# A four-layer attention stack on one core: more exponentials on VectorE in the last layer, and transposes and row sums in column strips

## The chip, the cores and the metric

The kernel runs on one core of a Trainium2 chip. TensorE (PE) multiplies matrices into PSUM, ScalarE (ACT) computes the exponentials, VectorE (DVE) copies, masks and scales, GpSimd (POOL) prepares weights and some masks, and DMA queues move data. The metric is the time of one execution on the device in microseconds. Before the change it is 2272.32 us, the median of three runs (2268.7 to 2274.12).

## The reference

Four layers, A, B, A, B, each with a residual. 2048 tokens, 640 features, 32 heads of 20. A looks at the last 256 keys, B at all keys.

```python
def layer(x, wqkv, wo, window):        # A: window = 256, B: none; S = 2048, D = 640, H = 32, Dh = 20
    h = (x - mean(x)) / sqrt(var(x) + 1e-5)
    q, k, v = split(h @ wqkv)           # each H x S x Dh
    scores = einsum("hqd,hkd->hqk", q, k) * Dh ** -0.5
    scores = where(allowed, scores, -1e9)   # A only
    p = softmax(scores)
    o = einsum("hqk,hkd->hqd", p, v)
    return x + o.reshape(S, D) @ wo
# x -> A -> B -> A -> B
```

The bulk of the work is the exponential of B's scores: 32 x 2048 x 2048 of them in each of two layers.

## The kernel before

**Tiling.** Queries go in four chunks of 512 (c = 0 to 3), heads in eight groups of four (g = 0 to 7). A *unit* is one layer, chunk and group, in the code (l, c, g) with l = 0 to 3. A *bank* is one PSUM bank of 128 x 512: the scores of one head j of the group for one block kc of 128 keys against the 512 queries. A B unit has 16 key blocks x 4 heads = 64 banks. Three banks (sometimes four) make a *tile*. For a tile t, TensorE writes the scores (L1305), ScalarE takes the exponential of the whole tile in one instruction (L1336), and two ticks later TensorE multiplies the result with the values (L1369) into the accumulator bank `op`. Score tiles alternate between PSUM banks 0 to 2 and 3 to 6, so TensorE can be one tile ahead of ScalarE and no more.

**The order is written out by hand.** A loop over t, one *tick* each, emits the scores, the exponential, then as much other work as a budget of credits allows (`pump`: layer norms, projections, value blocks, outputs, the tails of finished units), then the value matmuls. Each engine executes its own instructions in that order. Before a bank is reused, TensorE waits for its reader. Where TensorE would be too quiet, `keep_clock` adds filler matmuls of the identity with a mask (`unread`, L297), to keep its clock up.

**Column strips.** Most full-height matmuls are split by `by_columns` (L292 to L297) into four, each with 32 of the 128 stationary columns, so that they write four strips of 32 partitions. The profile shows their shape as 128\*32. Score matmuls use 32 rows (32\*128), value matmuls 21 columns (128\*21). Some steps use the whole width (128\*128): the transposes of the normed rows (L432, five for each 128 tokens, 300 in all), the row sums of finished units (L1042, eight for a pair of units), and a small transpose of their reciprocals (L1059, 128\*64).

**Exponentials on VectorE.** A unit can set a few banks *aside* (L678): VectorE computes them with bit operations and a polynomial (`t_side`, from L886), two banks (a *pair*) at a time: twice L909 (reads a score bank), L914, L919, L924, L928, L932, L940. In layer 1, from chunk 1 on, two banks of a unit are set aside; in layer 3, from (1, 1) on, four, which are the last key block of the four heads. In layer 3 their scores go to PSUM bank 6 by a matmul of their own (L902), on odd ticks when the side program asks for it. A tile of four banks uses bank 6 too, so it is only made when the side program does not. `SIDE_RATE` is the credit that the side program gets for each tile in the final stretch, 0.85; its steps cost 0.7 or 1.2 credits. Results go to buffers in `ka_all` that the last layer does not need otherwise (`side["out"]`), and their value matmuls (L1378) are the last of the unit. `side_need` (L972) and `side_done` (L990) make sure that the scores and the results are there in the program before they are used.

**Tail of a unit.** `finish_unit` copies `op` out (L856). For each pair of units `t_tail` sums the rows (L1042), takes reciprocals (L1047), splits them in two bf16 parts (L1051, L1052), transposes them (L1059, L1063), spreads them (L1080) and scales the outputs (L1084).

Of the kernel before, what the change touches and what calls it, by code (L numbers as in the profile page):

```python
# [9 lines left out]
BF16 = mybir.dt.bfloat16  # L10
# [5 lines left out]
P = 128  # L16
# [4 lines left out]
NT = S // P  # L21
KD = D // P
G = 8
C = 512
# [4 lines left out]
VW = DH + 1  # L29
# [4 lines left out]
LOG2E = 1.4426950408889634  # L34
EA, EB, EC, ED = -0.10468731, 1.17604568, 0.83196789, 0.24582313
KA = 18
SIDE_RATE = 0.85
QA = 4

PARTS = {  # L40
# [6 lines left out]
def kernel(  # L47
# [10 lines left out]
    nc = tc.nc  # L58
# [7 lines left out]
    big = pool("big", 1)  # L66
# [25 lines left out]
    ident = big.tile([P, P], BF16, name="ident", tag="ident")  # L92
# [6 lines left out]
    qts = [big.tile([P, C], BF16, name=f"qt{n}", tag=f"qt{n}") for n in range(4)]  # L99
    ka_all = big.tile([P, KA, C], BF16, name="ka", tag="ka")  # L100
    kas = [ka_all[:, n, :] for n in range(KA)]
    qas = [big.tile([P, C], BF16, name=f"qa{n}", tag=f"qa{n}") for n in range(QA)]

    ps = psp.tile([P, 8, C], F32, name="ps", tag="ps")
    op = ps[:, 7, :]
# [284 lines left out]
    def t_ln(l, c):  # L390
        while ("x", l, c) not in ready:
            yield ("wait", 1)
        yield from room("xnT", "ln")
        for n in (1, 0):
            order = worder[l, n]
            if order and not any(e in wtiles for e in order):
                wtiles[order[0]] = get_w(*order[0])
        users[l, c] = 9 if (l, c) == (0, 0) else (11, 12, 11, 11)[l]
        mv = mvs.pop((l, c))
        rstd = lnp.tile([P, 4], F32, name="rstd", tag="rstd")  # L400
        nc.gpsimd.tensor_scalar(  # L401
            out=rstd[:], in0=mv[:, :, 1], scalar1=EPS, scalar2=1.0, op0=ALU.add, op1=ALU.mult
        )
        nc.gpsimd.tensor_tensor(out=rstd[:], in0=rstd[:], in1=nhalf[:], op=ALU.pow)
        yield ("wait", 2)
        nmr = lnp.tile([P, 4], F32, name="nmr", tag="nmr")
        nc.vector.scalar_tensor_tensor(
            out=nmr[:], in0=mv[:, :, 0], scalar=-1.0, in1=rstd[:], op0=ALU.mult, op1=ALU.mult
        )
        xt = xtp.tile([P, KD, C], BF16, name="xnT", tag="xnT")  # L410

        def normed(i):
            xn = xnp.tile([P, D], BF16, name="xn", tag="xn")
            nc.vector.tensor_scalar(
                out=xn[:], in0=x_sb[:, 4 * c + i, :],
                scalar1=rstd[:, i : i + 1], scalar2=nmr[:, i : i + 1],
                op0=ALU.mult, op1=ALU.add,
            )
            return xn

        rows = deque([normed(0)])
        yield ("wait", 1)
        for i in range(4):
            if i < 3:
                rows.append(normed(i + 1))
            xn = rows.popleft()
            mb = yield from take_m()
            for _ in range(1+(l<2)):
                unread(mb)
            trp = ps[:, mb, :].bitcast(BF16)[:, 0 : KD * P].rearrange("p (c m) -> p c m", c=KD)  # L430
            for dc in range(KD):
                nc.tensor.transpose(  # L432
                    out=trp[:, dc, :], in_=xn[:, dc * P : (dc + 1) * P], identity=ident[:]
                )
            evac(xt[:, :, i * P : (i + 1) * P], trp)
            drop_m(mb)
            yield ("pe", 0.4)
        xnT[l, c] = xt
        live["ln"] -= 1
        ready.add(("xnT", l, c))  # L440
# [227 lines left out]
    class Unit:  # L668
        def __init__(self, l, c, g, part=None):
            self.l, self.c, self.g, self.part = l, c, g, part  # L670
            self.windowed = l % 2 == 0
            self.aside = ()
            if self.windowed:
                sets = [(m, b0, subs, j) for m, b0, subs in window_banks(c) for j in range(4)]
            else:

                if c > 0 and (l, c, g) != (3, 1, 0):
                    self.aside = (2, 3) if l == 1 else (0, 1, 2, 3)  # L678
                k0, k1 = key_blocks(l, part)
                sets = [  # L680
                    (None, 0, [(kc, 0, 4, 0)], j) for kc in range(k0, k1) for j in range(4)
                    if kc < NT - 1 or j not in self.aside
                ]
            n = len(sets)
            self.banks = [
                (self, j, m, b0, subs, i < 4, i >= n - 4 + len(self.aside), i == n - 1)
                for i, (m, b0, subs, j) in enumerate(sets)
            ]
# [179 lines left out]
    def side_start():  # L868

        assert live["xnT"] == 0  # L870
        tl = [xtp.tile([P, KD, C], BF16, name="xnT", tag="xnT") for _ in range(3)]
        live["xnT"] += 3
        f = [v[:, 0:4, :].rearrange("p a b -> p (a b)") for v in tl[0:3]]
        side["tiles"] = [v.bitcast(F32) for v in f]
        side["out"] = deque(ka_all[:, KA - 6 + 2 * n : KA - 4 + 2 * n, :] for n in range(3))
        side["late"] = True

    def side_early():
# [9 lines left out]
    def t_side():  # L888

        V = nc.vector  # L890
        while aside:
            u = aside[0]
            for pair in range(len(u.aside) // 2):
                while id(u) not in loaded or (u.l == 3 and not side["late"]):
                    yield None
                for i in range(2):
                    yield "bank"
                    xi, xm, xw = side["tiles"]
                    if u.l == 3:
                        mseq[0] += 1  # L900
                        mfree[6] = (state["tick"] + 2, mseq[0])
                        nc.tensor.matmul(  # L902
                            ps[:, 6, :], lhsT=u.k(NT - 1, u.aside[2 * pair + i]),
                            rhs=u.q(u.aside[2 * pair + i], 0, 4), start=True, stop=True,
                        )
                        side["psum"] = ps[:, 6, :]
                    scored = side.setdefault("scored", {})
                    scored[id(u)] = scored.get(id(u), 0) + 1
                    V.tensor_scalar(  # L909
                        out=xi.bitcast(I32)[:, i * C : (i + 1) * C], in0=side["psum"],  # L910
                        scalar1=SCALE * LOG2E * E23, scalar2=-128.0 * E23, op0=ALU.mult, op1=ALU.max,
                    )
                    yield 0.7
# [59 lines left out]
    def side_need(u):  # L973

        if u.l == 3:
            n = 0
            while u in aside and side.get("scored", {}).get(id(u), 0) < 4:
                n += 1
                assert n < 10000
                side["credit"] = max(side["credit"], 0.1)  # L980
                if side_step(mfree[6][0] <= state["tick"]):
                    continue
                t = choose(False)
                if t is None:
                    state["tick"] += 1
                else:
                    advance(t)
# [35 lines left out]
    def t_tail(us):  # L1023
# [15 lines left out]
        for i, (l, c, g, oT) in enumerate(us):  # L1039
            for qb in range(4):  # L1040
                a = 16 * i + 4 * qb
                nc.tensor.matmul(  # L1042
                    zp[:, a : a + 4], lhsT=oT[:, qb * P : (qb + 1) * P],
                    rhs=sel4[:], start=True, stop=True,
                )
        rz = rzp.tile([P, 2, 16], F32, name="rz", tag="rz")[:, 0:n, :]
        nc.vector.reciprocal(out=rz.rearrange("p u r -> p (u r)"), in_=zp)  # L1047
        drop_m(mb)
# [7 lines left out]
        mb = yield from take_m()  # L1056
        warm_bank(mb)
        rp = ps[0 : 32 * n, mb, :].bitcast(BF16)[:, 0:P]
        nc.tensor.transpose(  # L1059
            out=rp, in_=hl.rearrange("p u n r -> p (u n r)"), identity=ident[:]  # L1060
        )
        rT = rzp.tile([64, P], BF16, name="rT", tag="rT")
        nc.vector.tensor_copy(out=rT[0 : 32 * n], in_=rp)  # L1063
        drop_m(mb)
# [130 lines left out]
    with tc.manual_schedule():  # L1195
# [17 lines left out]
        while n < last_layer:  # L1213
            size = 2 if len(tiles) % 2 and narrow(banks[n][0]) else 3
            u = banks[n][0]
            at = placed.setdefault(id(u), [])
            extra = []
            if u.aside and len(at) < 2 and banks[n + 1][0] is u and len(tiles) >= 3 * len(at) + (at or [0])[0]:

                extra = [(u, u.aside[len(at)], "side", 0, [(NT - 1, 0, 4, 0)], False, False, False)]  # L1220
                at.append(len(tiles))
                size = 2
            for b in banks[n : n + size]:
                starts.setdefault(id(b[0]), len(tiles))
            tiles.append(banks[n : n + size] + extra)
            n += size
# [41 lines left out]
        while ended is None or t < ended + 8:  # L1268
# [84 lines left out]
            for n in range(2 if n_b == 0 or t > closed + 1 else 0):  # L1353
                u = pts[0][3][0] if pts else None
                size = 4
                if u is not None and u.aside and pts[0][3][4][0][0] == NT - 1:
                    size -= len(u.aside)
                if len(pts) < size or pts[size - 1][0] > t - n - (3 if u.windowed else 2):
                    break
                group = [pts.popleft() for _ in range(size)]  # L1360
# [13 lines left out]
                        )  # L1374
                if end and u.aside:
                    pair = side_done(u)
                    for n, j in enumerate(u.aside):
                        nc.tensor.matmul(  # L1378
                            op[32 * j : 32 * j + VW, :], lhsT=u.v(NT - 1, j),
                            rhs=pair[n // 2][:, n % 2, :], start=False, stop=True,  # L1380
                        )
                    side["out"].extend(pair)
                if end:
# [72 lines left out]
```

The softmax here doesn't subtract the row's maximum and nothing guards it: scores larger than these inputs give would overflow.

## Time and profile before

| | |
|---|---|
| time | 2272.32 us (2268.7 to 2274.12, three runs) |
| profiled run | 2268.72 us, span 2267.0 us |
| granted TensorE clock | 0.993 of full |
| exponentials on ScalarE (L1336) | 1636 instructions, 2089.3 us busy |
| VectorE's exponentials in layer 3 (L909 to L940) | 92 bank reads, 46 pairs |
| transposes of normed rows (L432) | 300, 28.4 us busy |
| row sums (L1042) | 512, 22.7 us busy |
| small transposes (L1059) | 64, 15.5 us busy |
| filler matmuls (L297, masks and ident) | 6452, 553.2 us busy |

A busy time of an engine counts each moment once, so matmuls that run side by side in four strips have a busy time well under their count times their mean. The page's slices divide the span in 40 equal parts of 56.7 us; layer 3 fills about the last thirteen.

### The profile page before, as it was taken

How to read it: one execution, taken by the hardware profiler on the slowest of the kernel's cores; microseconds unless marked ns; L12 is line 12 of the kernel's file. 1: busy time of each engine (PE TensorE's matmuls, PEld its weight loads, DVE VectorE, ACT ScalarE, POOL GpSimd, SP SyncE). 2: the span in 40 equal slices, each digit the busy share in tenths (PEclk: the TensorE clock that was granted, in tenths of full speed). 3: DMA queues.
4: the chain of work that ended last, by engine and by line, in shares of the span. 5: the costliest groups of instructions: out<-in, count | busy, mean ns of one | idle time of the engine just before them, and what ended most of it. 6: DMA issues, size and time to landing. Idle time of an engine off the chain costs nothing.

```text
span 2267.0 us, 65801 instructions
## 1 busy us (share of the span) xinstructions
PE 1973.3 (87%) x28523; PEld 776.0 (34%) x28524; DVE 1269.8 (56%) x2158; ACT 2166.5 (96%) x1740; POOL 326.2 (14%) x571
## 2 busy tenths in 40 slices
PE   8999998988888888888888988898888888888887
PEld 3444343334333333333333443342322222222222
DVE  6766575435554565555564644442566666656665
ACT  7789899999999989999899999999999999999998
POOL 4454334201100122001210022002000000000000
PEclk9999999999999999999999999999999999999999
DMA  6233223422210233002330033103211111111100
GB/s 195 72 91 94 74 87 93 100 76 50 78 34 15 60 88 104 17 28 58 93 90 15 16 106 105 31 17 91 65 51 31 31 40 34 31 31 43 42 21 16
DMA packets 88384, 136.80 MB, mean 60 GB/s; under 512 B 20766, under 2 KB 63486, under 8 KB 88094
## 3 DMA queue, kind: packets, MB, share of 16 engines
q1 hardware_dynamic: 68878, 79.43, 12.6%
q0 software_dynamic: 19216, 53.17, 8.0%
q8 instruction: 223, 3.65, 0.7%
q14 instruction: 67, 0.55, 0.1%
HBM read 99.52 MB, written 27.79 MB: 56 GB/s over the span
## 4 chain that ended last, share of the span: by engine, by line
ACT 49%; PE 23%; issue 17%; DVE 9%; POOL 1%; DMA 1%; SPq 0%; ACTq 0%; DVEq 0%; POOLq 0%
ACT pt L1336 47%; PE ps L297 14%; PE ps L1305 5%; PE ps L1369 2%; DVE pt L1416 1%; ACT ka L1336 1%; DVE x_sb L562 1%; DVE st L320 1%; DVE on L1084 1%; PE ps L432 1%; PE ps L1080 0%; DVE vs L320 0%; DVE va L320 0%; PE ps L1042 0%; DVE raw_o L909 0%
## 5 line engine op out<-in xcount | busy, mean ns | idle before, releaser
L1336 ACT ACTIVATE pt<-ps 128x1536 bf16<-128x1536 f32 (+2 forms) x1636 | 2089.3, 1462 | 64.8 <-PE ps L1305 56.2
L297 PE MATMUL ps<-masks,ident 128*32 128x512 bf16 x6452 | 553.2, 388 | 113.2 <-ACT pt L1336 59.1
L1305 PE MATMUL ps<-qt,kt 32*128 32x512 bf16 x4004 | 545.7, 384 | 85.5 <-ACT pt L1336 77.6
L1369 PE MATMUL ps<-pt,vt 128*21 128x512 bf16 x3844 | 392.2, 382 | 0.1
L1305 PEld LDWEIGHTS <-kt 32*128 32x128 bf16 x4004 | 163.4, 91 | 544.1 <-issue 526.8
L297 PEld LDWEIGHTS <-ident 128*32 128x32 bf16 x6452 | 162.0, 94 | 361.6 <-issue 350.4
L1416 DVE TENSOR_TENSOR pt<-pt,masks 128x1024 bf16<-128x1024 bf16 (+6 forms) x331 | 191.0, 604 | 154.9 <-ACT pt L1336 154.1
L297 PE MATMUL ps<-xnT,wqk 128*32 128x512 bf16 x3320 | 221.7, 385 | 17.1 <-DVE st L320 7.9
L320 DVE CAST st<-ps 128x512 bf16<-128x512 f32 x134 | 92.6, 691 | 188.1 <-PE ps L297 187.7
L909 DVE TENSOR_SCALAR xnT<-ps 128x512 int32<-128x512 f32 x92 | 63.6, 691 | 191.4 <-PE ps L902 191.3
L297 PE MATMUL ps<-wop,on 128*32 128x320 bf16 x3712 | 156.9, 301 | 13.3 <-DVE x_sb L562 8.4
L1305 PE MATMUL ps<-qa,ka 32*128 32x384 bf16 (+2 forms) x1408 | 117.9, 276 | 32.0 <-ACT pt L1336 29.4
L1369 PEld LDWEIGHTS <-vt 128*21 128x21 bf16 x3956 | 102.5, 91 | 110.4 <-issue 64.8
L1084 DVE TENSOR_TENSOR on<-on,ps 128x512 bf16<-128x512 bf16 x128 | 86.3, 683 | 67.0 <-PE ps L1080 65.3
L297 PE MATMUL ps<-wv,xnT 128*32 128x320 bf16 x2560 | 112.4, 301 | 10.8 <-DVE on L1084 3.3
L297 PEld LDWEIGHTS <-wqk 128*32 128x32 bf16 x3320 | 79.1, 96 | 112.8 <-issue 59.4
L562 DVE TENSOR_TENSOR x_sb<-x_sb,ps 128x320 bf16<-128x320 bf16 x120 | 58.0, 483 | 104.9 <-PE ps L297 104.7
L297 PEld LDWEIGHTS <-on 128*32 128x32 bf16 x3712 | 92.8, 96 | 65.9 <-issue 49.2
L856 DVE CAST on<-ps 128x512 bf16<-128x512 f32 x112 | 77.0, 687 | 59.9 <-PE ps L1378 32.9
L401 POOL TENSOR_SCALAR rstd<-mv 128x4 f32<-128x4 f32 x15 | 3.8, 253 | 712.4 <-DVE mv L388 702.8
L1305 PEld LDWEIGHTS <-ka 32*128 32x128 bf16 x1408 | 43.2, 92 | 117.0 <-issue 110.9
L1369 PE MATMUL ps<-pt,va 128*21 128x384 bf16 (+2 forms) x1408 | 76.9, 281 | 4.6 <-POOL pt L1406 3.5
(100 smaller groups left out, 1589.8 us busy)
## 6 DMA issues: line engine op xcount, KB each, us to landing
vt<-v_d SPq DMA_DIRECT2D x48, 336.0 KB
kt<-k_d SPq DMA_DIRECT2D x192, 80.0 KB
wqk<-in_B_wqkv_dram POOLq DMA_DIRECT2D x80, 160.0 KB, 3.6
wqk<-in_A_wqkv_dram POOLq DMA_DIRECT2D x70, 160.0 KB, 3.3
k_d<-st POOLq DMA_DIRECT2D x75, 128.0 KB, 2.2
q_d<-st POOLq DMA_DIRECT2D x75, 128.0 KB, 2.2
qt<-q_d SPq DMA_DIRECT2D x384, 20.0 KB
v_d<-vs POOLq DMA_DIRECT2D x16, 336.0 KB, 3.4
```

Of the source, the lines that this page charges most:

```text
L297: nc.tensor.matmul(out_[r], lhsT=lhsT[:, r], rhs=rhs, start=start, stop=stop)
L320: nc.vector.tensor_copy(out=out_, in_=in_)
L401: nc.gpsimd.tensor_scalar(out=rstd[:], in0=mv[:, :, 1], scalar1=EPS, scalar2=1.0, op0=ALU.add, op1=ALU.mult)
L432: nc.tensor.transpose(out=trp[:, dc, :], in_=xn[:, dc * P : (dc + 1) * P], identity=ident[:])
L562: nc.vector.tensor_tensor(out=xv, in0=had, in1=yp, op=ALU.add)
L856: nc.vector.tensor_copy(out=oT, in_=op)
L909: V.tensor_scalar(out=xi.bitcast(I32)[:, i * C : (i + 1) * C], in0=side["psum"], scalar1=SCALE * LOG2E * E23, scalar2=-128.0 * E23, op0=AL ...
L1084: nc.vector.tensor_tensor(out=oT, in0=oT, in1=zb, op=ALU.mult)
L1305: nc.tensor.matmul(sp[:, i, col * P : (col + qn) * P], lhsT=u.k(kc, j), rhs=u.q(j, q0, qn), start=True, stop=True,)
L1336: nc.scalar.activation(out=pt[:, i:k, b0 * P :], in_=sp[:, i:k, b0 * P :], func=ACT.Exp, scale=SCALE,)
L1369: nc.tensor.matmul(op[32 * j : 32 * j + VW, q0 * P : (q0 + qn) * P], lhsT=u.v(kc, j), rhs=pg[:, i, col * P : (col + qn) * P], start=(first ...
L1416: nc.vector.tensor_tensor(out=pt_[:, i:k, cols], in0=pt_[:, i:k, cols], in1=mv_, op=ALU.mult)
```

## The change

It has three parts. First, in layer 3, chunks 1 and 2, units with odd g set six banks aside in place of four: the two more are heads 0 and 1 of key block 14. Each of these eight units so has three pairs on VectorE. To make room in the order, the side program's credit for a tile goes from 0.85 to 1.1, and the four tiles `qa`, which become one tile `qa_all`, serve as two more result buffers. Second, the transposes of the normed rows are issued as four strips of 32 columns each, 20 for 128 tokens in place of five, and the small transpose as one strip for each unit. Third, the row sums go through `by_columns`, 32 narrow matmuls for a pair of units in place of eight.

```diff
-SIDE_RATE = 0.85
+SIDE_RATE = 1.1
...
-    qas = [big.tile([P, C], BF16, name=f"qa{n}", tag=f"qa{n}") for n in range(QA)]
+    qa_all = big.tile([P, QA, C], BF16, name="qa", tag="qa")
+    qas = [qa_all[:, n, :] for n in range(QA)]
...
             for dc in range(KD):
-                nc.tensor.transpose(
-                    out=trp[:, dc, :], in_=xn[:, dc * P : (dc + 1) * P], identity=ident[:]
-                )
+                for j in range(4):
+                    a = dc * P + 32 * j
+                    nc.tensor.transpose(
+                        out=trp[32 * j : 32 * j + 32, dc, :], in_=xn[:, a : a + 32],
+                        identity=ident[:],
+                    )
...
-                    self.aside = (2, 3) if l == 1 else (0, 1, 2, 3)
+                    self.aside = tuple((NT - 1, j) for j in ((2, 3) if l == 1 else range(4)))
+                    if l == 3 and (c < 3 and g % 2):
+                        self.aside += ((NT - 2, 0), (NT - 2, 1))
...
         side["out"] = deque(ka_all[:, KA - 6 + 2 * n : KA - 4 + 2 * n, :] for n in range(3))
+        side["out"].extend(qa_all[:, 2 * n : 2 * n + 2, :] for n in range(2))
...
-                nc.tensor.matmul(
-                    zp[:, a : a + 4], lhsT=oT[:, qb * P : (qb + 1) * P],
-                    rhs=sel4[:], start=True, stop=True,
-                )
+                by_columns(zp[:, a : a + 4], oT[:, qb * P : (qb + 1) * P], sel4[:], True, True)
...
-        nc.tensor.transpose(
-            out=rp, in_=hl.rearrange("p u n r -> p (u n r)"), identity=ident[:]
-        )
+        for i in range(n):
+            nc.tensor.transpose(
+                out=rp[32 * i : 32 * i + 32], in_=hl[:, i].rearrange("p n r -> p (n r)"),
+                identity=ident[:],
+            )
```

The rest of the diff carries the key block along with the head of a bank set aside, in the scores, in the count that `side_need` asks for and in the value matmuls.

More of the change, by code (lines that the diff above doesn't have):

```diff
@@ L677, in __init__ @@
                 if c > 0 and (l, c, g) != (3, 1, 0):
-                    self.aside = (2, 3) if l == 1 else (0, 1, 2, 3)
+                    self.aside = tuple((NT - 1, j) for j in ((2, 3) if l == 1 else range(4)))
+                    if l == 3 and (c < 3 and g % 2):
+                        self.aside += ((NT - 2, 0), (NT - 2, 1))
+                    if l == 1 and 0:
+                        self.aside += ((NT - 1, 0), (NT - 1, 1))
                 k0, k1 = key_blocks(l, part)
@@ L681, in __init__ @@
                     (None, 0, [(kc, 0, 4, 0)], j) for kc in range(k0, k1) for j in range(4)
-                    if kc < NT - 1 or j not in self.aside
+                    if (kc, j) not in self.aside
                 ]
@@ L901, in t_side @@
                         mfree[6] = (state["tick"] + 2, mseq[0])
+                        kc, j = u.aside[2 * pair + i]
                         nc.tensor.matmul(
-                            ps[:, 6, :], lhsT=u.k(NT - 1, u.aside[2 * pair + i]),
-                            rhs=u.q(u.aside[2 * pair + i], 0, 4), start=True, stop=True,
+                            ps[:, 6, :], lhsT=u.k(kc, j), rhs=u.q(j, 0, 4), start=True, stop=True
                         )
@@ L976, in side_need @@
             n = 0
-            while u in aside and side.get("scored", {}).get(id(u), 0) < 4:
+            while u in aside and side.get("scored", {}).get(id(u), 0) < len(u.aside):
                 n += 1
@@ L1217 @@
             extra = []
-            if u.aside and len(at) < 2 and banks[n + 1][0] is u and len(tiles) >= 3 * len(at) + (at or [0])[0]:
-                extra = [(u, u.aside[len(at)], "side", 0, [(NT - 1, 0, 4, 0)], False, False, False)]
+            if (
+                len(at) < len(u.aside) and banks[n + 1][0] is u
+                and len(tiles) >= 3 * len(at) + (at or [0])[0]
+            ):
+                kc, j = u.aside[len(at)]
+                extra = [(u, j, "side", 0, [(kc, 0, 4, 0)], False, False, False)]
                 at.append(len(tiles))
@@ L1355 @@
                 size = 4
-                if u is not None and u.aside and pts[0][3][4][0][0] == NT - 1:
-                    size -= len(u.aside)
+                if u is not None:
+                    size -= sum(kc == pts[0][3][4][0][0] for kc, _ in u.aside)
                 if len(pts) < size or pts[size - 1][0] > t - n - (3 if u.windowed else 2):
@@ L1376 @@
                     pair = side_done(u)
-                    for n, j in enumerate(u.aside):
+                    for n, (kc, j) in enumerate(u.aside):
                         nc.tensor.matmul(
-                            op[32 * j : 32 * j + VW, :], lhsT=u.v(NT - 1, j),
-                            rhs=pair[n // 2][:, n % 2, :], start=False, stop=True,
+                            op[32 * j : 32 * j + VW, :], lhsT=u.v(kc, j),
+                            rhs=pair[n // 2][:, n % 2, :], start=False,
+                            stop=all(jj != j for _, jj in u.aside[n + 1 :]),
                         )
```

## The prediction

> **What bounds the kernel now.** First the summary by engine and the slices of the span, to find the engine that is nowhere short of work.
>
> ```profile
> PE 1973.3 (87%) x28523; PEld 776.0 (34%) x28524; DVE 1269.8 (56%) x2158; ACT 2166.5 (96%) x1740; POOL 326.2 (14%) x571
> ...
> DVE  6766575435554565555564644442566666656665
> ACT  7789899999999989999899999999999999999998
> ```
>
> ScalarE (ACT) is full except in the first tenth of the span and in a few later slices. In the last third VectorE (DVE) is at six tenths: this is where it takes over exponentials. Next the stages (us, then busy time of PE, weight loads, DVE, ACT, POOL):
>
> ```profile
> 100.00:300.00 200.00, 184.42 (x3276) 85.46 (x3279) 129.58 (x259) 171.81 (x161) 85.47 (x157) 0.97 0.30 86
> ...
> 1530.00:1775.00 245.00, 207.86 (x2657) 69.84 (x2648) 123.23 (x167) 243.40 (x179) 14.02 (x20) 0.99 0.20 57
> 1775.00:2015.00 240.00, 204.21 (x2554) 64.08 (x2546) 148.45 (x185) 239.97 (x176) 0.00 (x0) 1.00 0.12 34
> 2015.00:2258.00 243.00, 206.88 (x2495) 65.51 (x2493) 149.27 (x190) 239.69 (x176) 0.00 (x0) 0.99 0.10 29
> ```
>
> The last three stretches are roughly chunks 1, 2 and 3 of the final layer. ScalarE is idle for 0.03 us of the 240 of chunk 2: there a microsecond less of exponentials is a microsecond less of time, if nothing else becomes late. From 100 to 300 us ScalarE is idle for 28 us and TensorE is busy for 184 of 200: there TensorE sets the pace. The list of waits names it: ScalarE's longest wait, over the whole span and then from 1600 to 2250 us, is for the score matmuls.
>
> ```profile
> ACT pt L1336 <- PE ps L1305: 56.2, 114, 2.2
> ...
> DVE xnT L909 <- PE ps L902: 191.3, 89, 5.2
> ...
> ACT pt L1336 <- PE ps L1305: 2.0, 5, 0.9
> ```
>
> The first line is the whole span, the other two the final layer. There ScalarE waits for only 2.0 us, and VectorE stands idle for 191 us before reading a score bank (L909), because the planner releases that step late and not because VectorE is short of time.
>
> **What the Trainium skill says.** "TensorEngine Tiling (Array Packing)", Key Properties: going from one tiling mode to another drains TensorE, going between tiles of one mode does not. The trace agrees:
>
> ```profile
> 758.91 0.40 PE L297 MATMUL ps<-masks,ident 128*32 128x512 bf16 x4
> 759.24 0.45 PE L432 MATMUL ps<-ident,xn 128*128 128x128 bf16 x5
> 759.63 0.40 PE L1369 MATMUL ps<-pt,vt 128*21 128x512 bf16 x4
> ...
> 1699.94 0.40 PE L297 MATMUL ps<-masks,ident 128*32 128x512 bf16 x4
> ...
> 1700.17 0.39 PE L1369 MATMUL ps<-pt,vt 128*21 128x512 bf16 x4
> ```
>
> Four column strips (128*32) are followed by other strips (128*21) after 0.23 us, but by a full-width transpose (128*128) after 0.33: a drain of 0.10 us. The five transposes hold TensorE for 0.39 us; at the 56 ns between their starts in the records they need 5 x 0.056 = 0.28, so the way back costs about 0.1 as well. "TensorE: Matmul & The Clock Gate", Part 3, says that matmuls on different strips run side by side, about 4 ns apart; Part 1 of that page ("Wait — 56ns, not 53.3ns?") says that starts never come closer than about 25 ns however narrow the matmul. For strips these two disagree. The trace speaks for the first at 128 columns:
>
> ```profile
> 703.18 0.39 PE L1369 MATMUL ps<-pt,va 128*21 128x384 bf16 x8
> 703.50 0.39 PE L1305 MATMUL ps<-qa,ka 32*128 32x384 bf16 x6
> ```
>
> Eight strips (four of 128 columns, four of 384, as window groups are built) took 0.32 us with the drain behind them, which is what one strip of 128 and one of 384 need. Nothing in the trace shows 32 strips of four columns in a row.
>
> **The change part by part.**
>
> *Fewer exponentials on ScalarE.* Units of chunks 1 and 2 with odd g, eight units, hand VectorE two more banks each, 16 banks. By the instruction order of both programs this removes two activations of 2048 columns, three of 1536 and one of 512, and adds one of 1024:
>
> ```profile
> L1336 ACT ACTIVATE pt<-ps 128x1536 bf16<-128x1536 f32 x1361 | 1875.1, 1560 | 56.5 <-PE ps L1305 49.7 <-issue 2.9 <-DVE on L1084 0.5
> ...
> L1336 ACT ACTIVATE ka<-ps 128x2048 bf16<-128x2048 f32 x28 | 56.0, 1998 | 0.0
> ```
>
> 2 x 1.998 + 3 x 1.560 + 0.680 - 1.068 = **8.3 us** (0.680 and 1.068 are the means of 512 and 1024 columns). All of it lies where ScalarE is never idle, so all of it counts. Four-bank tiles cost less per bank and become two fewer through the denser side work; that is in the sum.
>
> *More work on VectorE.* Eight more pairs. A pair is two bank reads (0.691), two bit operations (0.694) and four polynomial steps (1.22): 1.38 + 1.39 + 4.88 = 7.65 us, 61 us in all, over some 485 us of chunks 1 and 2. VectorE's 272 busy us there become 333, 69%. It has the time. The rate of 1.1 credits a tile (a credit is about a microsecond by these rows) against 1.56 us a tile leaves 0.46 us a tile for the 2 to 3 us of other work per unit of 20 tiles.
>
> *Lateness of the side results.* TensorE takes the pairs in the last matmuls of a unit (L1378), and behind that matmul stand the next score matmuls, for which ScalarE waits. In the program order the last step of a unit's last pair stands, before, 22 tiles ahead of that use in chunk 1 and 8 at the end of chunk 3. After, the reserve shrinks at odd units of chunk 2 to 4, 2, 1 and 0 tiles, then recovers in chunk 3. Only unit (2,7) is short: its last score is issued in tile 1470, its use ends tile 1473, some 3.6 tiles or 5.6 us later, while bank read, bit operations and polynomial need 0.69 + 1.39 + 4.88 = 7.0 us. TensorE stands about 1.4 us, of which the score tile in reserve (one activation, 1.56, less the tile's own TensorE work of about 0.9) hides half: **+0.8 us**, between 0 and 2.5.
>
> *Transposes in strips (L432, 60 groups of five become 20).* At 56 ns for four strips the groups keep their 0.28 us and lose the drains: all 60 follow strips, 45 precede strips, so 105 drains of 0.1, 10.5 us of TensorE. If starts were bound at 25 ns, 20 x 0.025 = 0.5 us would eat the gain. *The small transposes (L1059, 65)* lose a drain ahead 45 times and behind 51 times, 10 us. *Row sums (L1042, 65 groups)*: eight matmuls 25 ns apart become 32. Lower bound eight times 25 ns, a gain of up to two drains, 0.17 us a group; upper bound 32 x 0.025 = 0.8 us, a loss of 0.43. I take 0.3 to 0.4 us, no gain. What counts is only where ScalarE waits. Of the 60 transpose groups, 33 have a ScalarE gap within 4 us behind them; taking at most 0.2 us of it each, 6.3 us. The same count gives 16 and 2.5 us for the small transposes, 14 and 2.2 us for the row sums. Of the 8.8 us without row sums I take half, because a gap is often set by a chain of filler and projection matmuls that the next wait stretches again: **-4 us**.
>
> *At no cost:* one tile qa in place of four (the waits of its loads are the same in both programs), and 32 filler matmuls fewer among 6452.
>
> Sum: 2272.3 - 8.3 + 0.8 - 4 = 2260.8.
>
> **The rivals.**
> - *Only ScalarE's relief counts*: the TensorE time freed from drains turns into waits elsewhere (VectorE's evacuations, L320). For it: 27 of 60 transposes and 49 of 65 tails have no ScalarE gap behind them. 2272.3 - 7.5 = 2264.8.
> - *Everything counts*, as the time freed before 400 us adds up from group to group: 2272.3 - 8.3 - 9 = 2255.
> - *Strips are bound by issue*, 25 ns each: transposes gain nothing, row sums lose 0.43 us at the 15 places with a gap, 6.5 us. 2272.3 - 7.5 + 6.5 = 2271. Against it the eight strips above; for it, that the densest microsecond of the trace holds 68 TensorE instructions, and the new row sums would pass 64 in a third of that.
> - *VectorE becomes late*: L909 must free bank 6 before TensorE's next side score (L902), and TensorE is in order. If each of the 2 x 54 side scores of the final layer held the scores behind it by 0.12 us, 13 us: 2272.3 - 8.3 - 1 + 13 = 2276, and slower still, 2280, if the odd units' last pairs come late too. Against it: 31% of VectorE free.
>
> **How the numbers follow.** Forecast 0.54, only ScalarE 0.14, everything 0.13, issue-bound 0.11, VectorE late 0.08. The predicted time is 2261. The lower end, 2253, takes in the full gain; the upper, 2271, takes in the issue-bound case and leaves out late VectorE. Faster by over 0.2% means under 2267.8: the first three cases, 0.81, less 0.02 for the spread of 5 us between runs of before. Slower (over 2276.9): half of the last case and a little of the fourth, 0.06.
>
> **What would show it.** Right: in chunks 1 and 2 ScalarE stays over 99% busy and ends some 8 us sooner; VectorE near 69% there; next to no wait of L1378 for VectorE except near the end of chunk 2; the transposes follow fillers after 0.23 us. Wrong: row sums that hold TensorE for over 0.5 us; ScalarE waiting for scores in the final layer for more than 4 us; no fewer ScalarE gaps before 400 us.

## The result and the profile after

The changed kernel takes 2261.48 us (median of four runs, 2259.42 to 2264.71), before 2273.11 beside it: a ratio of 0.9954, with an interval of 0.9935 to 0.9973. In a second measurement on another chip (e11_after below) the ratio was 0.9977, 0.9967 to 0.9988. So the change is worth 5 to 10 us. The forecast was 2261. As the experiments show, this hit is luck: it is the sum of two large terms that were both wrong, in opposite directions.

The page's summary and slices of the changed kernel, in the order of those of before:

```profile
PE 1947.9 (86%) x30990; PEld 775.5 (34%) x30991; DVE 1328.4 (59%) x2222; ACT 2158.6 (96%) x1735; POOL 325.7 (14%) x571
...
DVE  6766675436464556455563644442577777776774
ACT  7789899999999999999899999999999999999998
```

VectorE gained 58.6 us of work, about what was worked out (61), and is now at seven tenths in the final layer. ScalarE lost 7.9 us. TensorE is busy for 25 us less with 2467 matmuls more: those are strips that run side by side and drains that are gone. The stages, with two stretches that hold about the same work as before (us, then PE, weight loads, DVE, ACT, POOL):

```profile
100.00:300.00 200.00, 183.47 (x3790) 88.25 (x3785) 133.09 (x267) 176.36 (x165) 87.39 (x160) 0.98 0.32 89
...
1765.00:2005.00 240.00, 204.40 (x2674) 63.32 (x2671) 178.65 (x218) 238.72 (x175) 0.00 (x0) 1.00 0.13 36
```

From 100 to 300 us ScalarE works 176.4 us, not 171.8: it is better fed. In chunk 2, where it lost 0.03 us of 240 before, it now loses 1.3 with less to do. The waits say the same. The first line is the whole span, the others are from 1600 to 2250 us:

```profile
ACT pt L1347 <- PE ps L1316: 58.0, 117, 2.5
...
DVE xnT L918 <- PE ps L912: 138.6, 95, 3.2
...
ACT pt L1347 <- PE ps L1316: 8.0, 13, 2.5
...
PE ps L1389 <- DVE ka L949: 2.6, 1, 2.6
```

In the final layer ScalarE waits 8.0 us for scores in place of 2.0, ahead of it 50.0 in place of 54.2 (58.0 - 8.0 against 56.2 - 2.0). A new line has come in: TensorE waits 2.6 us for the last polynomial step of one pair. To compare kernels I use one mark, the start of ScalarE's 1250th instruction (counted from zero, the load of its function table left out), just before the final stage; ScalarE's instructions up to it are the same in all kernels here. In the profiles of before and after it lies at 1583.8 and 1573.2 us, and from there to ScalarE's end it takes 672.1 and 674.0 us. In these two profiles all that was gained came ahead of the mark, and the stage for which the exponentials were taken away became 1.9 us longer.

### The profile page after: what moved, and what is told of

Same layout as the page of the kernel before. It is cut to its first block, busy times and chain, and to the rows that moved or that the text cites. A ratio compares the mean times of both kernels' runs of the same rounds, so it can differ in the third digit from the quotient of the medians.

```text
span 2258.4 us, 70795 instructions
## 1 busy us (share of the span) xinstructions
PE 1947.9 (86%) x30990; PEld 775.5 (34%) x30991; DVE 1328.4 (59%) x2222; ACT 2158.6 (96%) x1735; POOL 325.7 (14%) x571
## 4 chain that ended last, share of the span: by engine, by line
ACT 47%; PE 22%; issue 16%; DVE 13%; POOL 1%; DMA 1%; ACTq 0%; SPq 0%; DVEq 0%; POOLq 0%
ACT pt L1347 45%; PE ps L298 14%; PE ps L1316 5%; PE ps L1380 2%; DVE pt L1428 1%; ACT ka L1347 1%; DVE st L321 1%; DVE on L1092 1%; DVE x_sb L566 1%; DVE va L321 1%; PE ps L1088 1%; DVE xnT L937 1%; DVE xnT L933 1%; DVE xnT L941 0%; PE ps L435 0%
## 5 line engine op out<-in xcount | busy, mean ns | idle before, releaser
L298 PEld LDWEIGHTS <-ident 128*32 128x32 bf16 x6420 | 166.7, 94 | 363.1 <-issue 349.7
L298 PE MATMUL ps<-wop,on 128*32 128x320 bf16 x3712 | 156.9, 301 | 14.4 <-DVE x_sb L566 8.7
L918 DVE TENSOR_SCALAR xnT<-ps 128x512 int32<-128x512 f32 x108 | 74.7, 692 | 141.6 <-PE ps L912 138.6
L298 PEld LDWEIGHTS <-on 128*32 128x32 bf16 x5760 | 116.7, 95 | 76.9 <-issue 54.8
L298 PEld LDWEIGHTS <-xnT 128*32 128x32 bf16 x2560 | 63.7, 96 | 49.1 <-issue 38.0
```

What stands on the lines that cost most here:

```text
L298: nc.tensor.matmul(out_[r], lhsT=lhsT[:, r], rhs=rhs, start=start, stop=stop)
L918: V.tensor_scalar(out=xi.bitcast(I32)[:, i * C : (i + 1) * C], in0=side["psum"], scalar1=SCALE * LOG2E * E23, scalar2=-128.0 * E23, op0=AL ...
```

## The experiments

Percentages are against the kernel before on the same chip; us are the percentage of 2271. "Final" is the stretch from the mark to ScalarE's end in the profiled run, "idle" ScalarE's gaps in it, "waits" what TensorE waited for VectorE from 1585 to 2250 us, "half clock" how long the trace shows a granted TensorE clock of 0.5 in the final stretch.

| kernel | time against before, interval | us | final | idle | waits | half clock |
|---|---|---|---|---|---|---|
| before | | | 672.1 | 2.3 | 6.8 | 6.8 |
| after, first | -0.46% (-0.65, -0.27) | -10.4 | 674.0 | 9.4 | 19.5 | 13.6 |
| e11_after | -0.23% (-0.33, -0.12) | -5.2 | 675.5 | 10.3 | 19.3 | 20.4 |
| e1_strips | -0.37% (-0.55, -0.19) | -8.4 | 672.8 | 2.9 | 7.2 | 10.2 |
| e2_side | +0.02% (-0.09, +0.13) | +0.5 | 673.5 | 8.6 | 18.3 | 13.6 |
| e3_no_late | -0.38% (-0.51, -0.25) | -8.6 | 671.6 | 6.6 | 14.3 | 10.2 |
| e4_rate | +0.05% (-0.06, +0.17) | +1.1 | 681.5 | 9.8 | 14.4 | 25.7 |
| e5_trans | -0.30% (-0.40, -0.20) | -6.8 | 670.5 | 1.1 | 7.1 | 3.4 |
| e6_tails | -0.17% (-0.30, -0.05) | -3.9 | 671.6 | 2.0 | 7.4 | 7.1 |
| e7_hold | -0.35% (-0.50, -0.20) | -7.9 | 670.1 | 1.5 | 5.7 | 3.4 |
| e8_fill | -0.18% (-0.28, -0.08) | -4.1 | 675.8 | 4.6 | 11.1 | 3.4 |
| e9_c1_hold | -0.41% (-0.57, -0.26) | -9.3 | 672.2 | 5.1 | 10.2 | 13.6 |
| e10_gap | -0.77% (-0.99, -0.54) | -17.5 | 665.5 | 1.2 | 0 | 3.4 |
| e12_gap_only | -0.47% (-0.63, -0.30) | -10.7 | 671.5 | 1.9 | 0.2 | 6.8 |

Ahead of the mark the ten kernels with all the strips issue the same instructions in the same order on TensorE, VectorE and ScalarE, and yet their profiles reach it between 1571.0 and 1583.7 us. The granted clock goes with this spread: e1_strips, the earliest, has 10 us at half clock ahead of the mark, e9_c1_hold, the latest, 41. So one profile alone can't size the strips; for them the timed runs count. These spread in the same way: of the 34 runs of before beside e10_gap, the fastest (2263.5 us) has a mean granted clock of 0.996, the slowest (2279.4 us) 0.988. The final stage of four-bank kernels whose waits for VectorE are short (7.4 us or less) repeats within 3 us (670.1 to 672.8).

**Which part brought the gain: e1_strips, e2_side.** e1 is the kernel before with the diff's strips alone, e2 is the changed kernel with the strips undone:

```diff
# e1_strips, on before                      # e2_side, on after
+ four strips in t_ln (L432)                - four strips in t_ln
+ by_columns(zp...) in t_tail (L1042)       - by_columns(zp...)
+ one strip for each unit (L1059)           - one strip for each unit
```

> The kernel before with the strips alone (transposes, row sums and small transposes); the last layer's sharing of exponentials as before. Theory A (the strips brought nearly all of the gain: at one point of ScalarE's work, its 1250th instruction, the changed kernel is 10.6 us ahead, and after that it only loses): 2262 to 2263, 10 to 11 us under before, and the final layer from that point lasts 672 us as before. Theory B (the strips are worth the 4 us of the prediction, and the rest of the difference between the two profiles is the spread of runs): 2269.

> The kernel before with the sharing alone (six banks at odd units of chunks 1 and 2, rate 1.1, one qa tile), transposes and row sums full-width. Theory A (the ScalarE time saved is spent on stalls behind the late pair of unit (2,7) and its neighbours): 0 to 2 us over before, 2273 to 2275, with a ScalarE gap of about 2.5 us near the end of chunk 2 and TensorE's value matmuls of that unit waiting for VectorE. Theory B (the relief is worth its 7.5 us): 2265.5.

The strips give 8.4 us, the sharing nothing that can be measured (+0.5, between -2.0 and +3.0). Theory A holds in direction; it put the strips at 10 to 11 by one pair of profiles, two over the measured size but inside its interval (4.3 to 12.5). Two pairs of profiles with equal time at half clock ahead of the mark agree: e7_hold reaches it 7.6 us sooner than before (23.9 us at half clock in both), the changed kernel 7.4 us sooner than e2_side (17.1 in both). The sum of e1 and e2, -7.9, lies between the two measurements of the whole change. The strips do what the drains promised. In the changed kernel:

```profile
752.54 0.40 PE L298 MATMUL ps<-masks,ident 128*32 128x512 bf16 x4
752.76 0.45 PE L435 MATMUL ps<-ident,xn 128*32 128x128 bf16 x20
753.04 0.39 PE L1380 MATMUL ps<-pt,vt 128*21 128x512 bf16 x4
...
2038.25 0.40 PE L298 MATMUL ps<-masks,ident 128*32 128x512 bf16 x4
2038.47 0.39 PE L298 MATMUL ps<-sel,on 128*32 128x4 bf16 x32
2038.70 0.41 PE L1380 MATMUL ps<-pt,vt 128*21 128x512 bf16 x4
```

The start column is what to read. Fillers to transposes: 0.22 us, not 0.33. Twenty strips of a transpose group: 0.28, where the five full-width ones with their drain held 0.39. The 32 row sums with four columns each take 0.23 us, with no drain ahead of them (fillers to row sums 0.22). In the kernel before, the eight full-width ones took 0.28, and a drain of 0.1 ahead of them:

```profile
1046.43 0.40 PE L297 MATMUL ps<-masks,ident 128*32 128x512 bf16 x4
1046.76 0.35 PE L1042 MATMUL ps<-sel,on 128*128 128x4 bf16 x8
1047.04 0.40 PE L1369 MATMUL ps<-pt,vt 128*21 128x512 bf16 x4
```

**Transposes or tails: e5_trans, e6_tails.** Each is the kernel before with one of the two kinds of strips, the tails being row sums and small transposes.

```diff
# e5_trans: four strips in t_ln only
# e6_tails: by_columns(zp...) and one strip for each unit only
```

> The kernel before with the transposes of the normed rows alone in strips (L432). If gain follows the drains that lie where ScalarE waits: 60 groups save 105 drains of 0.1 us, 10.5 us of TensorE, of which the prediction's count gives 6.3 where a ScalarE gap follows; time 2264 to 2266, 5 to 6 under before, and the gain lies before 400 us of the span. If the prediction's half rate holds: 2267. If the small steps of the tails carry the strips' gain: 2269 to 2270.

> The kernel before with the row sums and the small transposes alone in strips (L1042, L1059). In the changed kernel's trace a row sum group holds 25 to 28 ns for four strips, so each group saves its drains, and the small transposes save theirs: some 19 us of TensorE, of which the gaps' count gives 4.7: 2265 to 2267. If the prediction's zero for row sums and half for the small transposes holds: 2269.

6.8 and 3.9 us; together 10.7, which agrees with e1's 8.4 within the intervals. For the transposes the count of gaps, not halved, gave 6.3. For the tails the interval, 1.1 to 6.8 us, holds the 4.7 of the count and the prediction's smaller figure (half of 2.5) alike. Where the gain lies is shown in part. From about 395 us (one and the same instruction of ScalarE) to the mark, e5's profile takes 1184.9 us and before's 1185.1, each with 3.4 us at half clock, so e5's gain, as far as these profiles show it, came earlier, as was expected. With all the strips that stretch takes 1181.1 us (the changed kernel) against 1184.6 (e2), without half clock in either. Why both kinds together gain there what neither does alone (e6 takes 1185.1, with 3.4 us at half clock) is open.

**Is it the one late pair: e3_no_late.**

```diff
-                    if l == 3 and (c < 3 and g % 2):
+                    if l == 3 and (c < 3 and g % 2) and (c, g) < (2, 7):
```

> The changed kernel, but unit (2,7) keeps four banks, so that its last pair is done 7 tiles ahead of its use and not 0; ScalarE takes two banks more, about 0.9 us. Theory A (the one late pair and the slow TensorE clock after it cost about 6 us): 2256 to 2257, 4 to 5 us under the changed kernel, 16 under before, and no wait of the side value matmuls for VectorE. Theory C (VectorE's denser queue costs the time throughout, by late tail steps such as the copy of the small transpose, L1071): 2261 to 2262, as the changed kernel.

This is the stall that the changed kernel shows near the end of chunk 2 (timeline of the changed kernel: start, us, engine, line; in brackets the idle time and who ended it):

```profile
2027.48 0.38 PE L1389 MATMUL ps<-ka,vt 128*21 128x512 bf16 x2
2027.97 1.22 DVE L941 SCALAR_TENSOR_TENSOR xnT<-xnT 128x1024 f32<-128x1024 f32 x1
2029.23 1.22 DVE L949 SCALAR_TENSOR_TENSOR ka<-xnT 128x1024 bf16<-128x1024 f32 x1
2030.51 0.39 PE L1389 MATMUL ps<-ka,vt 128*21 128x512 bf16 x2 [2.64 <-DVE ka L949]
2030.83 0.61 PE L1316 MATMUL ps<-qt,kt 32*128 32x512 bf16 x3
...
2031.55 1.45 ACT L1347 ACTIVATE pt<-ps 128x1536 bf16<-128x1536 f32 x1 [2.49 <-PE ps L1316]
```

TensorE stands 2.64 us before the side value matmuls, ScalarE 2.49 us behind it, and the scores that follow take 0.61 us in place of 0.39. The stretches show why (the column after POOL is the granted clock):

```profile
2020.00:2028.00 8.00, 7.30 (x90) 1.91 (x83) 5.16 (x7) 8.00 (x7) 0.00 (x0) 1.00 0.00 0
2028.00:2031.00 3.00, 0.49 (x5) 0.22 (x5) 2.49 (x3) 1.06 (x1) 0.00 (x0) 0.97 0.00 0
2031.00:2037.00 6.00, 6.00 (x46) 1.04 (x42) 2.86 (x5) 4.35 (x3) 0.00 (x0) 0.50 0.46 130
```

TensorE was busy for 0.5 us of three, and for the six us behind that its clock was at half, so that ScalarE went short three times more by about 0.48 us. That is 3.9 us without work for one late pair. Without it, the final stage is 671.6 us, 2 to 4 less than with it, but the time is that of the strips alone, some 6 us over what theory A expected. In the timed runs the late pair can't be told from noise: e3's -8.6 lies between the two measurements of the changed kernel (-10.4 and -5.2). The miss says that the late pair is only part: TensorE still waits 14 us for VectorE.

**Is it the pace: e4_rate, e7_hold, e8_fill.** e4 is the strips with the side rate 1.1, but four banks everywhere as before. e7 and e8 are e4 with one edit each:

```diff
# e7_hold
-                side_step(False)
+                if not (side["late"] and any(x.wake <= state["tick"] + 1 for x in tails)):
+                    side_step(False)
# e8_fill
-                state["least"] = (1.76 if state["unit"] >= woven else 1.0) * n_b / 3
+                state["least"] = (2.0 if state["unit"] >= index[3, 1, 1, None] else 1.76 if ...) * n_b / 3
```

> The kernel before with the strips and with the side rate 1.1, but four banks set aside everywhere as before: the pace without the extra work. No pair is late (19 tiles in reserve at every unit). Theory A: as the strips alone, within 1.5 us, 2261 to 2264. Theory C (the denser pace delays the tail steps behind polynomial steps and so costs time): 3 us or more over the strips alone.

> The strips, side rate 1.1, four banks set aside as in e4_rate; but in the final stretch the side program takes no step on a tick when a unit's tail may run on this or the next tick. No pair comes late (8 tiles or more in reserve at every unit but none at zero). Theory C (VectorE's tail steps stand behind polynomial steps, TensorE waits for them in order, goes quiet, its clock halves and ScalarE starves): the waits of TensorE for L1065 and L1086 in the final layer fall from 9 us to under 3, and the time falls to the strips' own, 2261 to 2263. Theory D (the pace costs for another reason, such as more reads of bank 6 or fewer four-bank tiles): stays within 3 us of e4_rate, 2267 to 2271.

> e4_rate with more filler matmuls in the final layer (the least activity of a tile 2.0 in place of 1.76, some 420 fillers of 512 columns more, 105 groups of four, 22 us of TensorE). If the halved clock is what turns VectorE's short delays into ScalarE's gaps: fewer stretches at half clock and 3 us or more under e4_rate, 2264 to 2267. If the delay itself is what costs, TensorE only has more to do: 2270 to 2275.

The pace alone, with no more work and no late pair, costs 9 us: e4's final stage is 681.5 us against 672.8, and its time loses all that the strips gave. ScalarE's tiles there are those of before (460 of three banks and 28 of four), and VectorE is busy for 60% of chunks 1 and 2 as before. A part of e4's timeline shows how (its lines 1065, 1086, 905 and 1307 are 1071, 1092, 912 and 1316 of the changed kernel):

```profile
1725.11 1.23 DVE L935 SCALAR_TENSOR_TENSOR xnT<-xnT 128x1024 f32<-128x1024 f32 x1
...
1726.25 0.21 DVE L1065 COPY rT<-ps 64x128 bf16<-64x128 bf16 x1
1726.39 1.21 DVE L943 SCALAR_TENSOR_TENSOR ka<-xnT 128x1024 bf16<-128x1024 f32 x1
1726.52 0.40 PE L297 MATMUL ps<-masks,ident 128*32 128x512 bf16 x4 [0.64 <-DVE rT L1065]
...
1728.25 0.54 PE L905 MATMUL ps<-qt,kt 32*128 32x512 bf16 x1 [0.35 <-DVE on L1086]
1728.72 0.61 PE L1371 MATMUL ps<-pt,vt 128*21 128x512 bf16 x4
...
1730.83 1.45 ACT L1338 ACTIVATE pt<-ps 128x1536 bf16<-128x1536 f32 x1 [1.37 <-PE ps L1307]
```

The stretches around it:

```profile
1722.00:1728.00 6.00, 5.04 (x93) 2.10 (x91) 5.90 (x10) 6.00 (x5) 0.00 (x0) 1.00 0.00 0
1728.00:1731.00 3.00, 2.75 (x20) 0.52 (x23) 0.89 (x2) 1.63 (x3) 0.00 (x0) 0.55 0.06 14
```

The small copy of the tail (L1065, 0.21 us) waits behind a polynomial step of 1.23 us, and so does the scaling (L1086) behind the next. Bank 6, which they read, is next written by TensorE, which stands 0.64 and 0.35 us, and then runs at half clock; ScalarE misses 1.37 us. It is no single case: e4 has six stretches at half clock behind the mark, five of them come within 7 us behind such waits, and 6.5 of the 8.1 us for which ScalarE waits for scores from 1585 to 2250 us lie around these five.

e7 keeps VectorE free when a tail is due: the waits fall from 14.4 to 5.7 us, the half clock from 26 to 3.4, the final stage to 670.1, the time back to the strips' own. e8 leaves most of the waits (11.1 us) and keeps TensorE busier: half clock 3.4 us, final stage 675.8, and about half of the loss is back, though TensorE has 420 matmuls more to do, 22 us by the estimate. The timed runs agree on the clock: its mean is 0.9899 over e4's 14 runs and 0.9919 over those of before beside them, 0.9935 over e8's 22 and 0.9918 over those of before. So the delay costs something by itself, and the halved clock behind it about as much again; as the fillers shortened the waits too, the split is rough.

**Is the relief to be had: e9_c1_hold, e10_gap, e12_gap_only.** e9 is the changed kernel with six banks in chunk 1 only, and e7's hold, limited to ticks when the side program works on a later unit than the one being computed. e10 is the changed kernel with six banks at six units, and it leaves VectorE's order alone and gives TensorE's a tick more:

```diff
# e9_c1_hold
-                    if l == 3 and (c < 3 and g % 2):
+                    if l == 3 and (c < 2 and g % 2):
# e10_gap
-                    if l == 3 and (c < 3 and g % 2):
+                    if l == 3 and (c < 3 and g % 2) and (c, g) < (2, 5):
...
-        mfree[b] = (state["tick"] + (not state["early"]), mseq[0])
+        mfree[b] = (state["tick"] + (not state["early"]) + side["late"], mseq[0])
...
-        yield ("wait", 2 if state["tick"] < last_tick[0] else 1)
+        yield ("wait", 2 if state["tick"] < last_tick[0] else 2)
```

e12 has e10's last two edits on e4, so with four banks. e11 is the changed kernel once more.

> The changed kernel with six banks only at the four odd units of chunk 1, and the side program held on ticks when a unit's tail may run on this or the next tick, as long as it works ahead of the unit being computed. Every pair is done 2 tiles or more ahead of its use. By the pitch of ScalarE's tiles (1.345 us for three banks, 1.76 for four) ScalarE has 3.7 us less than before. Theory C (tail steps behind polynomial steps, and late pairs, are what ate the relief): the final layer from ScalarE's 1250th instruction lasts 667 to 669 us, half clock under 7 us, time 11 to 13 us under before, 2258 to 2260. If the relief can't be had on this path at all: 2262 to 2264, as the strips alone.

> The changed kernel with six banks at six odd units (chunk 1, and (2,1) and (2,3)), and not with VectorE's order changed but TensorE's: bank 6 is used again one tick later after each reader in the final stretch, and a tail goes on one tick later after the small transpose. No pair is late by less than 1 tile; ScalarE has 4.5 us less than before. If it is TensorE's in-order wait for a late tail step that costs, time for it does as well as holding VectorE: its waits for L1071 and L1092 under 3 us, 10 to 13 us under before. If VectorE's order itself matters (the clock apart): 2262 to 2265.

> The changed kernel once more, beside the two others on one chip: 9 to 11 us under before, 2260 to 2262; the stall at the late pair of (2,7) and the half clock behind it again, the final layer from ScalarE's 1250th instruction 673 to 675 us.

> e10_gap without the extra banks: strips, side rate 1.1, four banks set aside as before, bank 6 used again one tick later after each reader and a tail one tick later after the small transpose. By ScalarE's tiles (1368 of three banks and 23 of four, against 1361 and 28) it has 0.6 us more than before, e10_gap 4.5 less. If e10_gap's final stage (665.5 us, 7 us under the strips alone) is the relief, shown once the stalls are away: here the final layer from ScalarE's 1250th instruction lasts 670 to 672, no wait of TensorE for VectorE's tail steps, 8 to 10 us under before. If the later use of bank 6 is itself the gain: 666 to 668, and 13 us or more under before. If the pace costs for another reason: 678 or more.

e9 missed: final stage 672.2 where 667 to 669 was expected, with 10.2 us of waits and 13.6 at half clock, and 9.3 us under before where 11 to 13 was expected. Its hold is lifted when the side program is short of time, so tails may come late there again; this wasn't traced. In its trace two of the three stretches at half clock (from 1903.8 and 2077.9 us) come right behind waits of TensorE for ScalarE, so that the clock halves without VectorE's delay too. e11 missed in time (5.2 us under before, not 9 to 11); the late pair, the wait of 2.6 us and the half clock behind it are there again. e10 is the best kernel of the study, 17.5 us under before (12 to 22) and 12 under the changed kernel beside it on the same chip (0.9923 against 0.9977, intervals apart). In its final layer no wait of TensorE for VectorE is left; these are all of TensorE's waits there, and below them ScalarE's only one:

```profile
PE ps L298 <- ACT pt L1347: 69.8, 165, 0.9
PE ps L298 <- ACT ka L1347: 7.5, 16, 0.8
PE ps L1316 <- ACT pt L1347: 4.3, 16, 0.4
PE ps L1380 <- ACT pt L1347: 1.4, 2, 0.9
...
ACT pt L1347 <- PE ps L1316: 1.1, 3, 0.5
```

TensorE waits for ScalarE alone. e12 has about the same final idle time (1.9 us against 1.2) and no relief, and takes 671.5 us there; e10 takes 665.5. Of the 6.0 us between them 5.3 are ScalarE's busy time (669.6 against 664.3): the twelve banks, for which the pitch of the tiles gives 5.1. So the profiles show that the relief is real and had been eaten. The times alone don't prove it: -17.5 and -10.7 were measured on two chips and their intervals overlap (-22.5 to -12.3, -14.3 to -6.8). e10 is faster than its expectation of 10 to 13 us; the strips' 8.4 and 7 of the final stage make 15, and with six timed runs the interval is wide. Its two changes of TensorE's order weren't tried apart.

## Why the prediction was right, and where it was not

- **By its own sign it was wrong**: it named more than 4 us of ScalarE waiting for scores in the final layer as a sign of being wrong, and there are 8.0. Its other signs for the strips hold (transposes follow fillers after 0.22 us, row sums hold TensorE for 0.23 us and not over 0.5).
- **What bounds the kernel**: right for both stages. ScalarE sets the final layer, TensorE the first 400 us.
- **Fewer exponentials, -8.3**: wrong in size. The records of two activations overlap, so their mean (1.560) is more than a tile costs. In before, the last tiles show the pitch:

```profile
2223.86 29.82 ACT L1336 ACTIVATE pt<-ps 128x1536 bf16<-128x1536 f32 x22
2253.44 2.01 ACT L1336 ACTIVATE ka<-ps 128x2048 bf16<-128x2048 f32 x1
2255.20 0.74 ACT L1336 ACTIVATE pt<-ps 128x512 bf16<-128x512 f32 x1
```

  22 tiles of three banks in 29.58 us are 1.345 each, the tile of four 1.76 to the next start. By these the sum is about 7 us, an estimate, as one tile of 512 and one of 1024 columns have no pitch here; ScalarE's busy time behind the mark fell by 5.1 us (669.8 to 664.7).
- **VectorE has the time**: this step failed, and it is the one that matters. In the runs the pace of 1.1 credits a tile alone cost 9 us (e4), and leaving VectorE free for the tails brought it back (e7). The share of 69% was right (305 us of 432 in the two stretches after the mark, 71%). But 0.46 us free a tile came from 1.56; from 1.345 it is 0.24, and with 1.22 us steps in a strict order the question was not the share but who stands behind a step. The rival "VectorE becomes late" named the mechanism, at bank 6, and I gave it 0.08; it happened at a smaller size, mostly on the tail's steps, and with a second cost that I had not seen, the clock.
- **Lateness, +0.8 at unit (2,7)**: the right unit, and the wait of 2.6 us against 1.4. It cost ScalarE 3.9 us without work, 2.5 behind the wait itself and 1.4 while the clock was at half behind it.
- **Transposes and tails, -4**: wrong in size. e1 shows 8.4. Halving the count had no support; the rival "everything counts" put this term at 9. The zero for row sums is not tested by itself, since e6 has them together with the small transposes; but the time that it rests on, 0.3 to 0.4 us for a group, was too long, as the trace shows 0.23. The 32 starts of such a group lie within 0.22 us, with the next four every 25 ns (median), so the Trainium skill's floor of 25 ns between starts ("TensorE: Matmul & The Clock Gate", Part 1, "Wait — 56ns, not 53.3ns?") holds here for a group of four strips, not for each.
- **At no cost**: the qa tile and the fewer fillers were not tried apart. e2 bounds them together with the sharing at 3.0 us.

The two wrong terms, 4.4 us too little for the strips and some 8 us too much for the sharing, leave the sum of e1 and e2 at -7.9 where -11.5 was forecast. The first measurement of the whole, -10.4, hides this; the second, -5.2, does not.

## What to carry to other kernels

When an engine off the critical path gets more work, ask first which short steps stand behind its long ones and who waits for those in order, and only then for its share of busy time. A buffer given back and a tail resumed one tick later can cure what a helper engine's long steps cause, as e10 did, at no cost in work. Price an instruction by its distance to the next start on a full engine, and check a forecast that came out right part by part before trusting its reasons.

## What the runs showed of the hardware

- Four strips side by side start 3 to 4 ns apart in the records (medians), with four columns and with 128 alike. Only the next four are spaced: 25 ns behind with four columns (32 matmuls in 0.23 us), 56 with 128.
- A change between strips and full width costs TensorE about 0.10 us each way. Taking it away at 60 transpose groups brought 6.8 us of kernel time (4.5 to 9.1, e5).
- Half clock came behind quiet stretches of TensorE, for 3.4 or 6.8 us in the final stage: in the 3.4 us ahead of each, TensorE was busy for at most three quarters, against 85% over the final layer of the changed kernel. It doesn't need a full stop: in e4, TensorE was busy for 5.0 of the six us ahead of the half clock at 1728 us. Nor is every quiet stretch followed by it: in before, TensorE was busy for 1.7 of the 3.4 us from 1872.1 us on, and the clock stayed at full. What decides was not found.
